# Second product of a two-layer block in seven quarter products, with v loaded through converting transfers

## The chip, the cores and the metric

The kernel runs on one core of a Trainium2 chip. A core has five engines that take their instructions in the order in which they were written and meet through semaphores: TensorE (PE in the profile; its weight loads are PEld), VectorE (DVE), ScalarE (ACT), GpSimd (POOL) and SyncE (SP), which here only issues transfers. The metric is the device time of one execution in microseconds (us). The kernel before took 211.14 us, the median of three runs (210.97 to 211.48).

## The reference, cut to what matters

A decayed linear attention over 4 sequences of 768 tokens with 8 heads of 64, in blocks of 64 tokens, and behind it a two-layer block (512 to 2048 to 512) with a sloped rectifier:

```
for b in range(nb):
    intra = einsum('bhic,bhjc->bhij', qb, kb) * Dmask
    intra = einsum('bhij,bhjd->bhid', intra, vb)
    inter = einsum('bhid,bhde->bhie', qb * lam_pow, kv_state)
    out[:, :, sl] = intra + inter
    kv_state = lam_block * kv_state + einsum('bhsd,bhse->bhde', kb * rev_pow, vb)
x = out.transpose(0, 2, 1, 3).reshape(B * S, H * D)     # 3072 x 512
h = x @ w_in                                            # 3072 x 2048
g = maximum(h, 0) + alpha * minimum(h, 0)
result = g @ w_out                                      # 3072 x 512
```

## The kernel before, in words

**Tiles.** The kernel works in blocks of 128 tokens instead of 64. The 3072 tokens are six chunks of 512 (two sequences by 256 tokens). Tokens of a chunk are kept by parity e (even or odd) and by sequence b, so a chunk is four groups of 128 tokens, (e, b). Attention is done in 24 units: unit n is a chunk, one of its two sequences, and one half of the heads, in that order, so units 8 to 11 belong to chunk 2 and units 16 to 19 to chunk 4.

**A unit's preparation.** `load` (line 80) brings k, q and v as fp32 into `raws`, `cast` (261) makes 16-bit copies, `key_decayed` (285) makes kdec = k times its decay, `transposes` with "D" (302) turns q and k in a transfer from SP, and `decayed` (346) makes qdT = turned q times its decay. For some units `load_v16` (272) brings v straight into 16 bits by a converting transfer that POOL issues.

**A unit's products** stand in `cluster(old, new)` (474). PE does `inter(old)` (4 products, which read qdT), `score_products(new)` (16), `intra(old)` (16, which read v16 and the masked scores) and `state_products(new)` (16 or 8, which read kdec and v16). Then DVE does `masked(new)` (398), ACT copies old's result to `XT`, which is the transposed x of the chunk (`attended`, 441), and DVE updates the state R (461). Each unit is new in one cluster and old in the next. `cluster2` (676) does the same for up to two old and two new units at once, with a second accumulator `acc2` in the PSUM bank "tk".

**The two-layer block.** `up(c, f)` (527) is one step of the first product: 4 matmuls of 512 columns give h for 128 of the 2048 hidden units and all 512 tokens of chunk c in a PSUM bank; ACT makes m = relu(-h) (540), DVE makes g = m * oma + h in fp16 (549). `down(c, t, part, 4)` (556) is a quarter of the second product for one 128-token group t: 4 matmuls of 512 columns, with g as the stationary operand and `w_out_sb` as the moving one. Behind the fourth part, `store` (573) copies the bank with ACT and writes 256 KB. A chunk has 16 ups and 16 downs.

**PSUM banks.** The 8 banks are acc (2), s (2), "op", "tk" and two that rotate under the name "h". Ups and downs name the bank they take. In the last stages ups take "h" alone, so an up can start only when DVE is done with the up two before.

**Order.** The emission order is written by hand. Lines 700 to 1003 interleave the ups and downs of chunks 0 to 2 with the preparation of units and with `cluster(n, n+1)` up to `cluster(15, 16)`. From line 1011 a `plan` gives for chunks 3, 4 and 5 a string of U (an up of that chunk) and D (a down of the chunk before), and at which step what else is emitted. I call these the stages of chunk 3, 4 and 5. Behind them `down_last` (580) does chunk 5's second product, with the last of its four groups cut into widths of 256, 128 and 128.

**Places that the steps below touch:** the clusters (11,12) in line 959 and (14,15) in line 991; the casts of v on ACT and POOL in lines 944 to 950, 966 and 998 to 1002; `key_decayed(12)` and `decayed(12)` in lines 937 and 938, the last work of POOL ahead of v of unit 13; the downs of chunk 1 in lines 915 to 930 and 987; the ups of chunk 2 from line 962; the plan; and `down_last`.

Of the kernel before, what the change touches and what calls it, by code (L numbers as in the profile page):

```python
# [11 lines left out]
def kernel(  # L12
# [16 lines left out]
    nc = tc.nc  # L29
# [9 lines left out]
    L = 128  # L39
# [10 lines left out]
    half_pool = ctx.enter_context(tc.tile_pool(name="half", bufs=4))  # L50
    kv_pool = ctx.enter_context(tc.tile_pool(name="kvh", bufs=8))
# [5 lines left out]
    o_pool = ctx.enter_context(tc.tile_pool(name="o", bufs=3))  # L57
# [22 lines left out]
    def load(c, bi, x, half=None, queue="S"):  # L80

        pb, b = c // 2, 2 * (c % 2) + bi
        if (c, bi) not in raws:
            raws[c, bi] = [raw_pool.tile([128, H, 2 * D], fp32, tag=f"{n}raw", name=f"{n}raw") for n in "kqv"]
        heads = ds(0, H) if half is None else ds(4 * half, 4)
        i = "kqv".index(x)
        (nc.gpsimd if queue == "G" else nc.sync).dma_start(
            out=raws[c, bi][i][:, heads, :],
            in_=(k, q, v)[i][b, heads, ds(pb * W, W), :].rearrange("h (p e) d -> p h (e d)", e=2),
        )  # L90
# [163 lines left out]
    def raw_of(n):  # L254
        c, bi, hh = units[n]
        return {
            x + "16": t[:, ds(4 * hh, 4), :].rearrange("p h (e d) -> p e h d", e=2)
            for x, t in zip("kqv", raws[c, bi])
        }

    def cast(n, name, eng):
        t = T.setdefault(n, {})
        if name == "v16":
            t[name] = kv_pool.tile([128, 4, 2, D], fp16, tag=name, name=name)
            c, bi, hh = units[n]
            copy_on(eng, t[name].rearrange("p h e d -> p h (e d)"), raws[c, bi][2][:, ds(4 * hh, 4), :])
            return
# [258 lines left out]

    def up(c, f, bi=None, bank="h"):
# [13 lines left out]
        if (c, f) not in G:  # L541
            G[c, f] = g_pool.tile([128, 2, 2, L], fp16, tag=f"g{f}", name=f"g{f}")
        g = G[c, f]
# [9 lines left out]
    def lhs(c, f, t):  # L553
        return G[c, f][:, t // 2, t % 2, :]
# [40 lines left out]
    acc2 = []  # L595

    def second():

        t = bank_of("tk", "acc2")
        nc.vector.memset(t[:, 256:512], 0.0)  # L600
        acc2.append(t)

    def out_of(i):
        x = [acc[:, 0, 0:256], acc[:, 1, 0:256]] if i == 0 else [acc2[0][:, 0:256], acc[:, 1, 256:512]]
        return [y.rearrange("p (h i) -> p h i", h=2) for y in x]

    def kv_of(i):
        return [kv_acc[0] if i == 0 else acc2[0][:, 256:512].rearrange("p (h l d) -> p h l d", h=2, l=2)]

    def inter_in(n, t, one_bank):  # L610
        co, bo, ho = units[n]
        pbo, bb = co // 2, 2 * (co % 2) + bo
        for a in range(2):
            for hp in range(2):
                nc.tensor.matmul(  # L615
                    t[a][:, hp, :].rearrange("p (e j) -> p e j", e=2),
                    lhsT=R[bb, ho, 2 * pbo + a][:, hp].rearrange("p l d -> p (l d)"),
                    rhs=T[n]["qdT"][:, :, hp, ds(a * 64, 64)],
                    start=(hp == 0 and not (one_bank and a == 1)),
                    stop=False,  # L620
                    skip_group_check=True,
                )

    def intra_in(n, t):
        for hp in range(2):
            for e in range(2):
                for hl, a in QUADS:
                    p = ds(a * 64, 64)
                    nc.tensor.matmul(  # L629
                        t[a][ds(hl * 64, 64), hp, :],  # L630
                        lhsT=T[n]["v16"][p, 2 * hp + hl, e, :],
                        rhs=T[n]["sm"][p, hl, hp, 1 - e, :],
                        start=False,
                        stop=(e == 1),
                        skip_group_check=True,
                    )

    def scores_in(n, s):
        t = T[n]
        for hp in range(2):  # L640
            for e in range(2):
                for a, hl in QUADS:
                    p = ds(hl * 64, 64)
                    nc.tensor.matmul(
                        s[hl][ds(a * 64, 64), hp, 1 - e, :].rearrange("p (e j) -> p e j", e=2),
                        lhsT=t["qkT"][p, 1, e, hp, ds(a * 64, 64)],
                        rhs=t["qkT"][p, 0, :, hp, ds(a * 64, 64)],
                        start=True,
                        stop=True,
                    )  # L650

    def masked_in(n, s):
        t = T[n]
        t["sm"] = sm_pool.tile([128, 2, 2, 2, L], fp16, tag="sm", name="sm")
        whole = mask_of(units[n][2])
        x = [list(y) for y in whole.ap]
        for hl in range(2):
            nc.vector.tensor_tensor(
                out=t["sm"][:, hl],
                in0=s[hl],  # L660
                in1=bass.AP(tensor=whole.tensor, offset=whole.offset + 384 * hl, ap=[x[0], [192, 2], x[2], x[3]]),
                op=ALU.mult,
            )

    def attended_in(n, t, eng):
        co, bo, ho = units[n]
        if co not in XT:
            XT[co] = xt_pool.tile([128, NHP, 2, 2, L], fp16, tag="xT", name="xT")
        x = XT[co][:, ds(2 * ho, 2), :, bo, :].rearrange("p h e (a j) -> p a (h e) j", a=2)
        if eng == "A":  # L670
            copy_on(eng, x, acc[:, :, 0:256].rearrange("p a (he j) -> p a he j", j=64))
        else:
            for a in range(2):
                copy_on(eng[a], x[:, a], t[a].rearrange("p h (e j) -> p (h e) j", e=2))

    def cluster2(olds, news):

        for i, n in enumerate(olds):
            inter_in(n, out_of(i), i == 1)
        if news:  # L680
            score_products(news[0])
        for i, n in enumerate(olds):
            intra_in(n, out_of(i))
        for i, n in enumerate(news):
            state_products(n, kv_of(i), i == len(olds))
        if len(news) == 2:
            s = [bank_of("h", "s2").rearrange("p (h x j) -> p h x j", h=2, x=2) for _ in range(2)]
            scores_in(news[1], s)
        if news:
            masked(news[0])  # L690
        if len(news) == 2:
            masked_in(news[1], s)
        for i, n in reversed(list(enumerate(olds))):
            attended_in(n, out_of(i), "A" if i == 0 else "AA")

    def states2(news):
        for i, n in enumerate(news):
            states(n, kv_of(i))
# [117 lines left out]
    load(4, 0, "v", 0)  # L816
# [275 lines left out]
```

## Time and profile before

| what | value |
|---|---|
| median of three runs | 211.14 us (210.97 to 211.48) |
| profiled execution, first to last instruction (span) | 209.1 us |
| TensorE clock granted, mean | 1.000 |
| matmul groups: up (line 532), down (562), last down (585) | 392, 320, 96 matmuls |
| data written to memory | 6.29 MB |

The profile shows one execution. The time of a run holds some two microseconds in addition to the span. Busy time of PE is from the start of a matmul to its modelled end; matmuls are pipelined, so the interval between two of them is shorter than the duration of one, and prices of PE work are taken from intervals. The chain of work is the sequence of instructions, followed back from the last one, each of which released the next. The timeline lists each engine's instructions in order of time, with neighbours of one kind merged: start, length, engine, line, operation and count.

### The profile page before, as it was taken

The numbers are of one execution on the slowest core, as the hardware profiler recorded it, in microseconds if no ns is written. First come the engines' busy times: TensorE is split into PE (matmuls) and PEld (weight loads), VectorE is DVE, ScalarE is ACT, GpSimd is POOL, SyncE is SP. The second block draws the span as 40 slices with busy tenths as digits, with TensorE's granted clock in tenths as the row PEclk, the third lists the DMA queues.
The fourth block names the chain that finished last, engine by engine and source line by source line (L and its number), as shares of the span: only waits on it lengthen the run. The fifth ranks groups of instructions, "written<-read, shape, count | busy, mean of one in ns | idle before, by whom it ended". The sixth has DMA issues, their size and how long they took to land.

```text
span 209.1 us, 5240 instructions
## 1 busy us (share of the span) xinstructions
PE 204.0 (98%) x2151; PEld 109.3 (52%) x2151; DVE 132.4 (63%) x233; ACT 110.8 (53%) x207; POOL 84.3 (40%) x114
## 2 busy tenths in 40 slices
PE   7999999999999999999999999999999999999993
PEld 6776455456445465555554464544544444444453
DVE  7978889488789466999956656744674344444000
ACT  7986778154876127666844544643454544344121
POOL 8999793052476983381902938022000000000000
PEclk9999999999999999999999999999999999999999
DMA  6999999998999998999199990404110100111113
GB/s 159 277 197 239 245 253 206 241 282 260 269 211 262 196 241 184 252 209 221 28 220 229 298 211 1 103 0 103 50 48 5 50 39 11 53 52 50 51 50 103
DMA packets 56716, 32.20 MB, mean 154 GB/s; under 512 B 22948, under 2 KB 53044, under 8 KB 56692
## 3 DMA queue, kind: packets, MB, share of 16 engines
q1 hardware_dynamic: 45764, 23.34, 46.4%
q0 software_dynamic: 10912, 8.52, 23.4%
q8 instruction: 17, 0.28, 0.6%
q14 instruction: 7, 0.06, 0.1%
q10 hardware_dynamic: 16, 0.00, 0.0%
HBM read 27.27 MB, written 6.29 MB: 161 GB/s over the span
## 4 chain that ended last, share of the span: by engine, by line
PE 92%; DVE 3%; ACT 2%; issue 1%; ACTq 0%
PE h_ps L532 39%; PE o_ps L562 33%; PE o_ps L585 7%; PE s L387 3%; PE acc L412 2%; PE tpx L337 2%; PE acc L371 2%; DVE dmask L200 1%; PE acc L432 1%; PE acc L629 1%; PE acc L615 1%; ACT qk L248 1%; ACT L178 1%; ACT xT L248 1%; DVE kdec L289 1%
## 5 line engine op out<-in xcount | busy, mean ns | idle before, releaser
L549 DVE SCALAR_TENSOR_TENSOR g<-m,oma,h_ps 128x512 f16<-128x512 f32 (+1 forms) x98 | 71.2, 736 | 46.3 <-ACT m L540 43.3
L532 PE MATMUL h_ps<-xT,w_in_sb 128*128 128x512 f16 (+1 forms) x392 | 91.4, 375 | 0.1
L540 ACT ACTIVATE m<-h_ps 128x512 f32<-128x512 f32 (+1 forms) x98 | 57.3, 588 | 51.0 <-PE h_ps L532 50.5
L562 PE MATMUL o_ps<-w_out_sb,g 128*128 128x512 f16 x320 | 79.0, 379 | 0.0
L532 PEld LDWEIGHTS <-w_in_sb 128*128 128x128 f16 x392 | 37.9, 98 | 43.6 <-issue 0.5
L562 PEld LDWEIGHTS <-g 128*128 128x128 f16 x320 | 29.9, 98 | 34.1 <-DVE g L549 0.2
L398 DVE TENSOR_TENSOR sm<-s,dmask 128x1024 f16<-128x1024 f32 x21 | 25.6, 1221 | 12.4 <-PE s L387 11.7
L351 POOL TENSOR_TENSOR qdT<-qkT,qdecay 128x512 f16<-128x512 f16 (+1 forms) x19 | 20.5, 1083 | 17.3 <-PE h_ps L532 7.2
L248 ACT ACTIVATE xT<-acc 128x512 f16<-128x512 f32 (+1 forms) x27 | 14.2, 550 | 22.6 <-PE acc L432 19.4
L575 ACT ACTIVATE o_sb<-o_ps 128x512 f32<-128x512 f32 (+2 forms) x26 | 14.7, 564 | 15.9 <-PE o_ps L585 10.9
L289 POOL TENSOR_TENSOR kdec<-kraw,kdecay 128x512 f16<-128x512 f32 x18 | 19.7, 1102 | 6.0 <-DMA kraw<-in_k_dram 6.0
L461 DVE SCALAR_TENSOR_TENSOR R<-R,rdecay,acc 128x128 f16<-128x128 f16 x54 | 15.3, 342 | 0.0
L252 POOL CAST qk<-qraw 128x512 f16<-128x512 f32 x12 | 7.4, 614 | 17.1 <-DMA qraw<-in_q_dram 16.2
L252 POOL CAST qk<-kraw 128x512 f16<-128x512 f32 x14 | 8.6, 614 | 13.9 <-DMA kraw<-in_k_dram 10.1
L585 PE MATMUL o_ps<-w_out_sb,g 128*128 128x512 f16 (+2 forms) x96 | 14.1, 308 | 0.0
L585 PEld LDWEIGHTS <-g 128*128 128x128 f16 x96 | 8.1, 98 | 6.1
L387 PE MATMUL s<-qkT 64*64 64x128 f16 x336 | 8.8, 221 | 0.1
L276 POOL DMA_DIRECT2D v<-in_v_dram x11 | 8.6, 792 | 0.0
L248 ACT ACTIVATE qk<-qraw 128x512 f16<-128x512 f32 x11 | 6.9, 624 | 2.7 <-DMA qraw<-in_q_dram 2.1
L252 POOL CAST v<-vraw 128x512 f16<-128x512 f32 x10 | 6.1, 615 | 5.4 <-DMA vraw<-in_v_dram 5.4
L387 PEld LDWEIGHTS <-qkT 64*64 64x64 f16 x336 | 5.8, 106 | 2.1 <-issue 0.4
L248 ACT ACTIVATE qkT<-tpx 128x512 f16<-128x512 f16 x11 | 6.5, 598 | 0.8 <-PE tpx L337 0.8
(76 smaller groups left out, 133.5 us busy)
## 6 DMA issues: line engine op xcount, KB each, us to landing
out_dram<-o_sb SPq DMA_DIRECT2D x23, 256.0 KB, 2.3
kraw<-in_k_dram SPq DMA_DIRECT2D x7, 512.0 KB, 5.6
qraw<-in_q_dram SPq DMA_DIRECT2D x6, 512.0 KB, 5.9
w_in_sb<-in_moe_w_in_dram POOLq DMA_DIRECT2D x4, 512.0 KB, 8.0
w_out_sb<-in_moe_w_out_dram POOLq DMA_DIRECT2D x4, 512.0 KB, 10.6
vraw<-in_v_dram SPq DMA_DIRECT2D x7, 256.0 KB, 5.7
qraw<-in_q_dram POOLq DMA_DIRECT2D x6, 256.0 KB, 7.2
qraw<-in_q_dram SPq DMA_DIRECT2D x6, 256.0 KB, 4.8
```

The source lines that it names most:

```text
L248: nc.scalar.activation(out, in_, AF.Copy)
L252: nc.gpsimd.tensor_copy(out=out, in_=in_)
L289: engine(eng).tensor_tensor(out=kdec, in0=kr, in1=kdecay[:, ds(4 * hh, 4), :].rearrange("p h e -> p e h").unsqueeze(3).to_broadcast([128, ...
L351: engine(eng).tensor_tensor(out=qdT[:, :, :, p], in0=(t["qps"] if eng == "P" else t["qkT"][:, 0])[:, :, :, p], in1=qdecay[:, hh, :, :, p], ...
L387: nc.tensor.matmul(t["s"][ds(a * 64, 64), hl, hp, 1 - e, :].rearrange("p (e j) -> p e j", e=2), lhsT=t["qkT"][p, 1, e, hp, ds(a * 64, 64)] ...
L398: nc.vector.tensor_tensor(out=t["sm"].rearrange("p a h x j -> p (a h) x j"), in0=t["s"].rearrange("p a h x j -> p (a h) x j"), in1=mask_of ...
L461: nc.vector.scalar_tensor_tensor(out=R[b, hh, m + 1][:, hp], in0=R[b, hh, m][:, hp], scalar=rdecay[:, 2 * hh + hp : 2 * hh + hp + 1], in1= ...
L532: nc.tensor.matmul(h_ps[:, 0:n] if bi is None else h_ps[:, 0:n].rearrange("p (e j) -> p e j", e=2), lhsT=w_in_sb[:, gi, ts(f, 128)], rhs=x ...
L540: nc.scalar.activation(m[:, 0:n], h_ps[:, 0:n], AF.Relu, scale=-1.0)
L549: nc.vector.scalar_tensor_tensor(out=g, in0=mv, scalar=oma[:, f : f + 1], in1=hv, op0=ALU.mult, op1=ALU.add)
L562: nc.tensor.matmul(o_ps, lhsT=lhs(c, f, t), rhs=w_out_sb[:, f, :], start=(f == 0), stop=(f == NF - 1),)
L585: nc.tensor.matmul(o_ps[:, 0:n], lhsT=lhs(c, f, t), rhs=w_out_sb[:, f, ds(x, n)], start=(f == 0), stop=(f == NF - 1),)
```

## The change

Chunks 2 to 5 form their second product from quarters. With A the 512 tokens by 2048 hidden values (rows cut by parity e, columns into f below 8 and from 8 on) and B the weights (rows cut likewise, columns into halves of 256), the scheme takes four sums of quarters of A, four sums of quarters of B, seven products instead of eight, and adds products in PSUM: a bank is read between two products that accumulate in it.

- **Sums of weights** (`weight_sum`): eight DVE instructions of 128x1024 fp16, two for each sum. Six are emitted among the first downs of chunk 1, two behind the last down of chunk 1. The last sum overwrites a quarter of `w_out_sb`.
- **Sums of g** (`g_sum`): sixteen instructions of 128x512 fp16 for each chunk. Sums 1 and 3 go to POOL (`sums13`) during the ups, 2 and 4 to DVE during the downs. In the last chunk the sums 2 are emitted behind the second part of product 1.
- **Products** (`product`): each of the seven has two parts (b), each of 8 matmuls with 256 moving columns. A D of the plan is now one such part, 14 for a chunk.
- **Readouts** (`evacuated`): four copies on ACT and three additions on DVE for a chunk, where four ACT copies stood.
- **Order:** ups of chunks 2 to 5 go by f = 0, 8, 1, 9 and so on. `cluster2` goes, and all units use `cluster`. The plan is one string for the chunks 3 to 5.
- **v:** the fp32 loads of v and the casts go. Where a cast of v stood, `load_v16` stands, on POOL.

```diff
-    o_pool = ctx.enter_context(tc.tile_pool(name="o", bufs=3))
+    o_pool = ctx.enter_context(tc.tile_pool(name="o", bufs=5))
...
     def casts(n, eng):
-        for name, e in zip(("k16", "q16", "v16"), eng):
+        for name, e in zip(("k16", "q16"), eng):
             cast(n, name, e)
+        load_v16(n)
         key_decayed(n)
...
+    def weight_sum(i, part):
+        p = ds(4 * part, 4)
+        (b11, b12), (b21, b22) = [[y[:, p] for y in x] for x in halves]
+        w = [w_sum[:, x, p] for x in range(3)]
+        out, in0, in1 = [(w[0], b12, b11), (w[1], b22, w[0]), (w[2], b21, w[1]), (b12, b22, b12)][i]
+        nc.vector.tensor_tensor(out=out, in0=in0, in1=in1, op=ALU.subtract)
...
+    def g_sum(c, i, j, eng):
+        a11, a12, a21, a22 = [part_of(c, j, half, e) for e in range(2) for half in range(2)]
...
+        out, in0, in1, op = {
+            1: (s1, a21, a22, ALU.add),
+            3: (a21, a11, a21, ALU.subtract),
+            2: (a11, s1, a11, ALU.subtract),
+            4: (a12, a12, a11, ALU.subtract),
+        }[i]
+        engine(eng).tensor_tensor(out=out, in0=in0, in1=in1, op=op)
+
+    CHAIN = [(1, 0), (2, 1), (6, 0), (5, 1), (7, 0), (3, 1), (4, 0)]
+
+    def product(c, i, b, t, fresh, last, cols):
+        for f in range(NF // 2):
+            x = sums[c][:, f, b] if i == 5 else g_of(c, f + 8 * (i in (2, 3, 4)))[:, int(i in (4, 7)), b]
...
+            nc.tensor.matmul(
+                t[:, cols],
+                lhsT=x,
+                rhs=w,
+                start=(fresh and f == 0),
...
+    def evacuated(c, i, key, t, b=None):
...
+        where = {2: ("c11", 0, 0), 3: ("c12", 0, 1), 4: ("c21", 1, 0), 7: ("c22", 1, 1)}
+        if i in (1, 5, 6, 4):
+            nc.scalar.activation(fresh({1: "c11", 5: "c22", 6: "c12", 4: "c21"}[i]), t, AF.Copy)
+        else:
+            o = X[where[i][0]]
+            nc.vector.tensor_tensor(out=o, in0=o, in1=t, op=ALU.add)
...
+    def down2(c, x):
+        i, side = CHAIN[x // 2]
+        b = x % 2
...
+        product(c, i, b, t, b == 0 and i in (1, 2, 5), i in (2, 3, 4) and b == 1, ds(256 * b, 256))
+        if b == 1:
+            evacuated(c, i, "w", t)
...
+    def down2_last(c):
+        order = [(i, side, b) for i, side in CHAIN[:5] for b in range(2)]
+        order += [(3, 1, 0), (4, 0, 0), (3, 1, 1), (4, 0, 1)]
...
+            product(c, i, b, t, i in (1, 2, 5), i in (2, 3, 4), ds(0, 256))
+            evacuated(c, i, b, t[:, 0:256], b)
+            if i == 1 and b == 1:
+                for j in range(4):
+                    g_sum(c, 2, j, "V")
...
+    def sums13(c, j, eng="G"):
+        g_sum(c, 1, j, eng)
+        g_sum(c, 3, j, eng)
...
     down(1, 1, 0, 4, "h")
+    weight_sum(0, 0)
     transposes(11, "D", False)
     down(1, 0, 0, 4, "tk")
+    weight_sum(0, 1)
...
     cluster(10, 11, "A")
-    load(3, 1, "v", 0)
-    cast(13, "v16", "A")
+    load_v16(13)
     down(1, 2, 2, 4, "h")
-    cast(12, "v16", "A")
+    load_v16(12)
     transposes(13, "D", False)
-    cast(15, "v16", "G")
+    load_v16(15)
...
     cluster(13, 14, "A")
     down(1, 3, 3, 4, "op")
+    weight_sum(3, 0)
+    weight_sum(3, 1)
+    up(2, 4, None, "h")
+    up(2, 12, None, "h")
+    up(2, 5, None, "op")
+    cluster(14, 15, "A")
...
+        3: {
+            0: lambda: (turned(18), load(5, 0, "k"), load(5, 0, "q"), decayed(17)),
+            2: lambda: prepared(19),
+            4: lambda: cluster(16, 17),
+            7: lambda: (turned(19), decayed(18)),
+            10: lambda: prepared(20),
+            11: lambda: cluster(17, 18),
...
+    order = "UU" + "DU" * 14
...
+                up(c, u // 2 + 8 * (u % 2), None, "h")
+                u += 1
+                if x in (17, 21, 25, 29):
+                    sums13(c, (x - 17) // 4)
             else:
-                down(c - 1, d // 4, d % 4, 4)
+                down2(c - 1, d)
+                for i, j in {1: [(2, 0), (2, 1)], 2: [(2, 2)], 3: [(2, 3)], 5: [(4, 0)], 6: [(4, 1)], 7: [(4, 2)], 8: [(4, 3)]}.get(d, []):
+                    g_sum(c - 1, i, j, "V")
                 d += 1
-    for t in range(4):
-        down_last(NC - 1, t, (DM,) if t < 3 else (256, 128, 128))
+    down2_last(NC - 1)
```

More of the change, by code (lines that the diff above doesn't have):

```diff
@@ L593, in down_last @@
             x += n
[L595 to L650, printed above, removed]
@@ L676, in cluster2 @@
[L676 to L694, printed above, removed]
```

211 lines of the change are left out of this document (106 added, 105 removed).

## The prediction

> **What bounds the kernel now.** I read the page's busy time and chain of work first, then the stretches by window, then the chain's pieces in order of time.
>
> ```profile
> PE 204.0 (98%) x2151; PEld 109.3 (52%) x2151; DVE 132.4 (63%) x233; ACT 110.8 (53%) x207; POOL 84.3 (40%) x114
> DVE  7978889488789466999956656744674344444000
> PE 92%; DVE 3%; ACT 2%; issue 1%; ACTq 0%
> ```
>
> TensorE sets the time: it is busy for 98% of the span and makes up 92% of the chain. DVE has room on average, but not everywhere: its row has four nines in slices 17 to 20. Each slice is 5.2 us, so these are about 84 to 105 us.
>
> ```profile
> 82.00:106.00 24.00, 23.94 (x293) 12.47 (x292) 22.58 (x43) 16.14 (x28) 12.56 (x15) 1.00 0.82 177
> 162.00:192.00 30.00, 30.00 (x169) 13.85 (x170) 12.81 (x18) 13.77 (x25) 0.00 (x0) 1.00 0.09 36
> ```
>
> These are a stretch's length, PE, PEld, DVE, ACT and POOL busy, clock, DMA share and GB/s. From 82 to 106 us, the first product of chunk 2, DVE works 22.58 of 24 us. From 162 to 192 us, where chunk 5's ups alternate with chunk 4's downs, it works 12.81 of 30. So whatever takes matmul columns away is gained, as long as nothing else becomes late, and the first of these stretches is where that is hardest.
>
> **What the seven products save.** From the chain (start, length) and from ACT in the timeline:
>
> ```profile
> 190.30 0.86 PE o_ps L562 x4
> 191.16 0.86 PE h_ps L532 x4
> 192.03 13.91 PE o_ps L585 x96
> 206.01 0.28 ACT o_sb L575
> ```
>
> ```profile
> 202.47 0.60 ACT L575 ACTIVATE o_sb<-o_ps 128x512 f32<-128x512 f32 x1 [2.91 <-PE o_ps L585]
> 204.22 0.38 ACT L575 ACTIVATE o_sb<-o_ps 128x256 f32<-128x256 f32 x1 [1.15 <-PE o_ps L585]
> 205.12 0.28 ACT L575 ACTIVATE o_sb<-o_ps 128x128 f32<-128x128 f32 x1 [0.51 <-PE o_ps L585]
> ```
>
> A down and an up last 0.864 us each, 216 ns for a matmul of 512 columns. The three copies mark the ends of the 512, 256 and 128 wide pieces of the last group: 16 matmuls of 256 columns took 204.22 - 202.47 = 1.75 us, 109.4 ns each. A chunk's second product is now 16 x 0.864 = 13.82 us. It becomes 14 parts of 8 matmuls, 112 x 109.4 ns = 12.25 us. Chunks 2 to 4 save 3 x 1.57 = 4.71 us, and the last second product, 13.91 us in the chain, saves 1.66. **Together -6.4 us**, on an engine that is never idle.
>
> **Clusters, one at a time.**
>
> ```profile
> 86.42 0.22 PE acc L371 x4
> 87.34 0.97 PE o_ps L562 x4
> 123.22 0.45 PE acc L615 x8
> 124.93 1.83 PE o_ps L562 x8
> ```
>
> `cluster` with one old and one new unit takes 0.92 us of PE (86.42 to 87.34), `cluster2` with two and two 1.71 (123.22 to 124.93), or 0.86 for a pair. The last stages handle 7.5 pairs: 7.5 x 0.06 us, **+0.5 us**.
>
> **v of unit 12.** `cluster(11, 12)` reads it in its state products. Today ACT casts it from data long loaded. The change issues its transfer on POOL, in order behind `decayed(12)` and the transfer for unit 13.
>
> ```profile
> 75.89 1.16 POOL L351 TENSOR_TENSOR qdT<-qkT,qdecay 128x512 f16<-128x512 f16 x1
> 76.99 0.61 POOL L252 CAST v<-vraw 128x512 f16<-128x512 f32 x1
> ```
>
> ```profile
> L276 POOL DMA_DIRECT2D v<-in_v_dram x11: 752/780/912, 5.1 to 60.7; - x11
> DMA to landing us min/median/max: 4.9/6.4/11.2
> ```
>
> ```profile
> 80.84 0.29 PE L432 MATMUL acc<-v,kdec 64*64 64x64 f16 x16
> ```
>
> The cast that follows `decayed(12)` starts at 76.99, so today's POOL would issue unit 13's transfer there and unit 12's 0.78 later. Two things move this. Without the loads of v on SP, a wait of POOL for q at 67.96 shrinks (below). Against it, six weight sums on DVE fall into 69 to 75 us, beside POOL's own work:
>
> ```profile
> 67.96 0.61 POOL L252 CAST qk<-qraw 128x512 f16<-128x512 f32 x1 [1.70 <-DMA qraw<-in_q_dram]
> 68.53 1.90 POOL L289 TENSOR_TENSOR kdec<-kraw,kdecay 128x512 f16<-128x512 f32 x1
> 44.53 1.04 POOL L289 TENSOR_TENSOR kdec<-kraw,kdecay 128x512 f16<-128x512 f32 x1 [1.04 <-DMA kraw<-in_k_dram]
> ```
>
> ```profile
> 68.84 0.69 DVE L289 TENSOR_TENSOR kdec<-kraw,kdecay 128x512 f16<-128x512 f32 x1
> 44.56 1.30 DVE L250 CAST qk<-kraw 128x512 f16<-128x512 f32 x1
> 36.46 0.41 DVE L250 COPY qkT<-tpx 128x512 f16<-128x512 f16 x1
> ```
>
> The POOL product takes 1.04 us by itself and 1.90 when DVE's product of two SBUF operands runs inside it. The DVE cast beside a POOL product takes 1.30, and a DVE copy of that size out of PSUM 0.41. So the two engines delay each other by up to one instruction. The wait for q can give back 1.7 us at most, and six sums of about 0.6 us (next part) can cost 3.7. I take +1.0: unit 12's transfer starts at 76.99 + 1.0 + 0.78 = 78.8. The shortest landing of the eleven, 4.9 us, fits best, as the queue is then shorter than on average: 83.7 against 80.84, and I take **+2.7 us**. A quiet queue or an earlier issue ends it at 0; the full 3.7 us of delay and the median landing would make it 76.99 + 3.7 + 0.78 + 6.4 - 80.84 = 7.0. PE waits there in the middle of a cluster, and everything behind it on PE waits too.
>
> **Sums of weights behind the last down of chunk 1.** Two sums of 128x1024 fp16 enter DVE's busiest stretch. The price is not in the trace. Nearest rows:
>
> ```profile
> 35.52 0.68 DVE L289 TENSOR_TENSOR kdec<-kraw,kdecay 128x512 f16<-128x512 f32 x1
> 36.12 0.42 DVE L351 TENSOR_TENSOR qdT<-qkT,qdecay 128x256 f16<-128x256 f16 x1
> ```
>
> ```profile
> L250 DVE COPY qkT<-tp 128x1024 f16<-128x1024 f16 x1 | 0.7, 686 | 0.0
> ```
>
> The next instruction starts 0.60 us after the product of 512 (36.12 - 35.52), which has an fp32 operand, and 0.34 after that of 256: 1.12 for 1024 at this rate. Copies of fp16 alone took 0.41 for 512 and 0.69 for 1024, and the next one starts 0.08 before such a row ends (35.52 + 0.68 against 36.12). That gives 0.34 and 0.61. These are the two ends; I take the copies' rate, as all operands of the new sums are fp16 too.
>
> ```profile
> 94.40 2.40 DVE L549 SCALAR_TENSOR_TENSOR g<-m,oma,h_ps 128x512 f16<-128x512 f32 x3
> 96.71 1.22 DVE L398 TENSOR_TENSOR sm<-s,dmask 128x1024 f16<-128x1024 f32 x1
> 97.84 1.11 DVE L461 SCALAR_TENSOR_TENSOR R<-R,rdecay,acc 128x128 f16<-128x128 f16 x4
> 98.88 2.72 DVE L549 SCALAR_TENSOR_TENSOR g<-m,oma,h_ps 128x512 f16<-128x512 f32 x4
> 103.15 0.74 DVE L549 SCALAR_TENSOR_TENSOR g<-m,oma,h_ps 128x512 f16<-128x512 f32 x1
> ```
>
> ```profile
> 100.77 0.98 PE h_ps L532 x4
> ```
>
> From 94.40 to 103.9 DVE hardly rests, so 2 x 0.61 us make all that follows late. The g of chunk 2's last up ends at 105.1 instead of 103.9 and the g of chunk 3's first up at 105.9. The third up of chunk 3 needs that bank. Counted from 100.77, three ups and a down later, it would start at 104.2. **+1.7 us** (0.4 if the sums were free, 2.7 at the upper price, 4.8 if each also met a POOL product).
>
> **Sums of g in stages 3 to 5.** Product 6 starts with the fifth D and reads sum 2 of its last group in its seventh matmul. DVE makes that sum behind the g of the up before and the addition that reads product 2.
>
> ```profile
> 192.70 0.75 DVE L549 SCALAR_TENSOR_TENSOR g<-m,oma,h_ps 128x512 f16<-128x512 f32 x1 [0.98 <-ACT m L540]
> ```
>
> The last up ends at 192.03 (191.16 + 0.86) and its g starts 0.67 later. Call the end of such an up 0: its g takes DVE to 1.42, the addition (priced as g, 0.75) to 2.17, the sum to 2.51. PE has a D, an up and six matmuls to do, 0.87 + 0.86 + 0.66 = 2.39, less 0.2 for the weight load ahead. So PE waits about 0.35 us, once in each stage. In the stage of chunk 3, POOL is occupied by `prepared(19)`, `decayed(17)` and the late sums 1 and 3, and DVE's four sums and POOL delay each other: I add 0.8 (0, or 3.4 if each of the four met a whole product of 1.04 and 0.8 of that were absorbed). **+1.15, +0.35, +0.35 us.** The other sums and the four ACT copies have several D of cover; if DVE fell a microsecond behind, they would be late next.
>
> **The end.** Behind the last up, g (to 1.43), two POOL sums of 1.04 and a DVE sum of 0.34 must pass before product 6's seventh matmul at 3.5 + 0.66 - 0.2 = 3.96 us: about even, up to 1 us late when DVE's sums stretch POOL's. The last piece has 256 columns instead of 128, a copy of 0.38 instead of 0.28 us and twice the bytes. **+0.5 us** together (0.2 to 1.2).
>
> **Sum.** -6.4 + 0.5 + 2.7 + 1.7 + 1.15 + 0.7 + 0.5 = +0.85 us on the profiled 209.1. The median of the runs stands 2.04 above the span, so 211.14 + 0.85 = **212.0 us**. The additions are of the size of the gain, and I do not know their sign better than that.
>
> **Rivals.**
>
> *v lands in time.* The place is the state products of `cluster(11, 12)` at 80.84, the price is the 2.7 us, and it decides when unit 12's transfer is issued before 76 (with 4.9 us of landing). For it speaks that POOL's wait of 1.70 for q gets shorter, as the loads of v on SP go; against it, the weight sums beside POOL. Not slower, but faster: **209.3 us**.
>
> *Everything hides.* v lands, and the DVE sums cost PE nothing but the lag of 0.4 at the third up and the 0.35 of each stage: 209.3 - 1.3 - 0.8 - 0.3 = **206.9 us**. Against it stands DVE's 22.58 of 24 us.
>
> *DVE and POOL block each other.* Each DVE sum of two SBUF operands meets a POOL product, and one of them pays: 2.3 us more at `cluster(11, 12)`, 1.0 more at the weight sums, 1.6 more in the stage of chunk 3: **216.9 us**. For it: the rows of 1.90 and 1.30 us. Against it: the DVE product inside the 1.90 took 0.69, no more than alone, and POOL is busy for 12.56 of the 24 us from 82 to 106, so not each sum meets it. [...]
>
> *Halving the columns saves nothing,* because the weight loads, one for each matmul, set the pace: then a chunk's second product stays at 13.8 us and the time is 212.0 + 6.4 = **218.4 us**. Against it: the 128 wide pieces, also with a load each, took 205.12 - 204.22 = 0.90 us for 16, 56 ns. [...]
>
> **Chances.** Forecast (211.0 to 214) 0.35; v in time 0.27; everything hides 0.13; blocking 0.21; no saving on PE 0.04. About 0.3%, 0.6 us, is what a measurement of this kernel can tell from no change. Faster: 0.13 + 0.27 = 0.40. The same: 0.11, the forecast's lower part. Slower: 0.49. The range leaves out the last case and the outer ends of "hides" and "blocking": 206.5 to 217.5 us. By itself the forecast has 211 to 214.
>
> **What would show it.** Right: 256 wide matmuls at 109 ns intervals; a gap of PE in the middle of `cluster(11, 12)` that ends with the landing of v; a wait of PE at the third up of chunk 3 that ends with DVE's g; a short wait at product 6 of each chunk that ends with DVE's sum. Wrong: PE without gaps from 75 to 115 us (then 207), or gaps that end with POOL's sums 1 and 3, or with v of unit 17, whose transfer also stands late in POOL's order.

## The result and the profile after

The changed kernel takes 220.49 us (median, 217.51 to 220.88), beside 211.08 for the kernel before on the same chip: ratio 1.0405, interval 1.0336 to 1.0473. It is slower, and 3 us above the upper end of the range. The profiled execution has a span of 218.3 us, 9.2 more than before.

The page of the changed kernel, the same rows as before: busy time, DVE's slices, the granted clock by slice, and the chain.

```profile
PE 201.9 (92%) x2311; PEld 127.8 (59%) x2311; DVE 166.1 (76%) x284; ACT 110.0 (50%) x203; POOL 129.7 (59%) x149
DVE  7988889287889974999965879757879548585840
PEclk9999999999999999999996999999999999999999
PE 68%; DVE 9%; POOL 6%; issue 6%; DMA 6%; ACT 3%; ACTq 0%; SPq 0%; DVEq 0%; POOLq 0%
```

PE works less than before (201.9 us after 204.0), but idles for 16.4 us of the span, where it idled for 5.1. DVE has 34 us more work and POOL 45. The chain, 92% PE before, is PE for 68% only. The row of the clock has one slice at 6, the 22nd, about 115 to 120 us.

PE's timeline, only its waits and what follows the longest: start, length, instruction, count, and in brackets the idle time before it and what ended it.

```profile
78.34 0.38 PE L368 MATMUL acc<-qdT,R 128*128 128x128 f16 x4 [2.06 <-DVE R L458]
...
84.31 0.32 PE L429 MATMUL acc<-v,kdec 64*64 64x64 f16 x16 [1.41 <-DMA v<-in_v_dram]
...
101.32 3.61 PE L538 MATMUL h_ps<-xT,w_in_sb 128*128 128x512 f16 x16 [1.53 <-DVE g L553]
...
108.71 1.04 PE L643 MATMUL o_ps<-w_out_sb,g 128*128 128x256 f16 x8
110.40 1.02 PE L538 MATMUL h_ps<-xT,w_in_sb 128*128 128x512 f16 x4 [0.66 <-DVE g L553]
...
115.37 0.31 PE L429 MATMUL acc<-v,kdec 64*64 64x64 f16 x8 [3.16 <-DMA v<-in_v_dram]
115.62 1.89 PE L643 MATMUL o_ps<-w_out_sb,g 128*128 128x256 f16 x8
117.30 1.88 PE L538 MATMUL h_ps<-xT,w_in_sb 128*128 128x512 f16 x4
119.00 1.04 PE L643 MATMUL o_ps<-w_out_sb,g 128*128 128x256 f16 x8
...
120.75 1.04 PE L643 MATMUL o_ps<-w_out_sb,g 128*128 128x256 f16 x8
121.62 1.03 PE L538 MATMUL h_ps<-xT,w_in_sb 128*128 128x512 f16 x4
...
123.76 0.39 PE L643 MATMUL o_ps<-w_sum,g 128*128 128x256 f16 x2 [0.45 <-DVE g L626]
...
145.17 1.02 PE L538 MATMUL h_ps<-xT,w_in_sb 128*128 128x512 f16 x4 [0.60 <-DVE g L553]
...
155.42 0.39 PE L643 MATMUL o_ps<-w_sum,g 128*128 128x256 f16 x2 [0.60 <-DVE g L626]
...
176.49 1.02 PE L538 MATMUL h_ps<-xT,w_in_sb 128*128 128x512 f16 x4 [0.60 <-DVE g L553]
...
206.40 1.60 PE L643 MATMUL o_ps<-w_sum,g 128*128 128x256 f16 x12 [0.46 <-DVE g L626]
```

From here the 9.2 us can be put together. A D, eight matmuls of 256 columns, takes 121.62 - 120.75 = 0.87 us, as forecast, so PE's -6.4 stands; the clusters' +0.5 is taken over as forecast. The ten waits sum to 11.5 us. The D at 115.62 and the up at 117.30 take 119.00 - 115.62 = 3.38 us instead of 0.87 + 0.86, another 1.65. That makes 7.3. PE also loses a little more at each wait than the brackets say: the D at 108.71 is through at 109.58, the next up starts at 110.40, 0.82 later and not 0.66. If each of the ten waits costs some 0.16 more, as this one does, that is 1.6 (an estimate), which makes 8.9 of the 9.2.

Three places carry most of it, and none of them has a term in the sum of the prediction: `cluster(10, 11)` at 78.34, v of unit 17 at 115.37, and the slow stretch behind it.

**At cluster(10, 11)** PE waits for the state R of the cluster before. DVE's timeline of the changed kernel shows why:

```profile
70.98 5.05 DVE L609 TENSOR_TENSOR w_sum<-w_out_sb,w_sum 128x1024 f16<-128x1024 f16 x4
75.95 1.21 DVE L395 TENSOR_TENSOR sm<-s,dmask 128x1024 f16<-128x1024 f32 x1
77.09 1.10 DVE L458 SCALAR_TENSOR_TENSOR R<-R,rdecay,acc 128x128 f16<-128x128 f16 x4
```

Four sums of weights take 5.05 us, 1.26 each, and the masking and R of the cluster stand behind them. POOL casts and multiplies without a pause at that time. How much room DVE had is in its timeline of the kernel before:

```profile
73.61 1.22 DVE L398 TENSOR_TENSOR sm<-s,dmask 128x1024 f16<-128x1024 f32 x1 [3.42 <-PE s L387]
```

DVE rested for 3.42 us ahead of this masking, and R was done at 75.86 for a cluster that PE began at 76.44, so some 4.0 us were to spare. Six sums at the prediction's 0.61 us would have fitted. The six as they ran held DVE for 6.2 us (69.12 to 70.32 and 70.98 to 75.95), 2.2 too much, about the wait.

The first two of them ran beside a cast of POOL, in DVE's and POOL's timelines of the changed kernel:

```profile
69.12 1.28 DVE L609 TENSOR_TENSOR w_sum<-w_out_sb 128x1024 f16<-128x1024 f16 x2
68.44 2.43 POOL L253 CAST qk<-qraw 128x512 f16<-128x512 f32 x1 [0.86 <-DMA qraw<-in_q_dram]
```

Here POOL paid, 2.43 us for a cast that takes 0.61 elsewhere, although it had started first, and the two sums took 0.68 each, as they do where POOL waits. Beside the other four both paid: two casts of POOL took 1.07 and two qdT 1.60, where 0.61 and 1.16 are usual.

**At 115.37** the chain in order of time (start, length, what) runs through transfers:

```profile
98.70 6.04 DMA kraw<-in_k_dram
...
104.81 1.05 POOL kdec L285
105.86 1.11 POOL s L626
...
109.27 6.06 DMA v<-in_v_dram
...
115.37 0.31 PE acc L429 x8
```

POOL stands still for a load of k, then makes kdec, two sums of g and a qdT, and only then issues v of unit 17 (109.27), which lands 6.06 us later.

**Behind that wait** the clock falls. The stretches by window of the changed kernel (length, five engines' busy time, granted clock, DMA share, GB/s):

```profile
114.00:116.00 2.00, 0.63 (x10) 0.48 (x10) 0.00 (x0) 0.28 (x1) 1.98 (x4) 0.90 1.17 322
116.00:118.00 2.00, 2.00 (x10) 1.22 (x8) 1.65 (x3) 0.78 (x2) 2.00 (x3) 0.50 1.97 221
118.00:120.00 2.00, 2.00 (x12) 1.19 (x11) 1.46 (x3) 0.74 (x2) 1.98 (x3) 0.75 1.15 106
```

PE gets half its clock (0.50 granted from 116 to 118 us) from about the end of the wait to about 119 us and pays 1.65 us beyond the wait itself.

### The profile page after: what moved, and what is told of

The parts are those of the page before. It is cut to its first block, busy times and chain, and to the rows that moved or that the text cites. A ratio compares the mean times of both kernels' runs of the same rounds, so it can differ in the third digit from the quotient of the medians.

```text
span 218.3 us, 5673 instructions
## 1 busy us (share of the span) xinstructions
PE 201.9 (92%) x2311; PEld 127.8 (59%) x2311; DVE 166.1 (76%) x284; ACT 110.0 (50%) x203; POOL 129.7 (59%) x149
## 4 chain that ended last, share of the span: by engine, by line
PE 68%; DVE 9%; POOL 6%; issue 6%; DMA 6%; ACT 3%; ACTq 0%; SPq 0%; DVEq 0%; POOLq 0%
PE h_ps L538 29%; PE o_ps L643 20%; PE o_ps L566 7%; DMA v<-in_v_dram 3%; DMA kraw<-in_k_dram 3%; DVE w_sum L609 3%; PE s L384 3%; PE unread L151 2%; PE acc L409 2%; PE tpx L334 2%; DVE g L626 2%; ACT m L546 2%; DVE g L553 2%; POOL s L626 2%; PE acc L368 2%
## 5 line engine op out<-in xcount | busy, mean ns | idle before, releaser
L643 PEld LDWEIGHTS <-g 128*128 128x128 f16 x384 | 37.2, 99 | 14.6 <-DVE g L626 2.9
L626 POOL TENSOR_TENSOR s<-g 128x512 f16<-128x512 f16 x16 | 18.8, 1175 | 39.6 <-PE o_ps L643 24.2
L643 PE MATMUL o_ps<-w_out_sb,g 128*128 128x256 f16 x256 | 33.2, 277 | 0.0
L249 ACT ACTIVATE xT<-acc 128x512 f16<-128x512 f32 x24 | 14.3, 597 | 31.8 <-PE acc L429 29.4
L566 PE MATMUL o_ps<-w_out_sb,g 128*128 128x512 f16 x128 | 30.4, 380 | 0.0
L626 POOL TENSOR_TENSOR g<-g 128x512 f16<-128x512 f16 x16 | 19.1, 1197 | 1.3
L272 POOL DMA_DIRECT2D v<-in_v_dram x24 | 18.8, 787 | 0.0
L643 PE MATMUL o_ps<-w_sum,g 128*128 128x256 f16 x128 | 17.2, 273 | 1.5 <-DVE g L626 1.5
L566 PEld LDWEIGHTS <-g 128*128 128x128 f16 x128 | 11.4, 98 | 12.0 <-DVE g L553 0.2
L673 ACT ACTIVATE o_sb<-o_ps 128x512 f32<-128x512 f32 (+1 forms) x20 | 10.2, 512 | 14.1 <-PE o_ps L643 13.6
L626 DVE TENSOR_TENSOR g<-s,g 128x512 f16<-128x512 f16 x16 | 10.8, 704 | 0.0
```

Source lines behind the costliest of these rows:

```text
L272: nc.gpsimd.dma_start(out=v16.rearrange("p h e d -> p h (e d)"), in_=v[2 * (c % 2) + bi, ds(4 * hh, 4), ds((c // 2) * W, W), :].rearrange( ...
L566: nc.tensor.matmul(o_ps, lhsT=lhs(c, f, t), rhs=w_out_sb[:, f, :], start=(f == 0), stop=(f == NF - 1),)
L626: engine(eng).tensor_tensor(out=out, in0=in0, in1=in1, op=op)
L643: nc.tensor.matmul(t[:, cols], lhsT=x, rhs=w, start=(fresh and f == 0), stop=(last and f == NF // 2 - 1), skip_group_check=True,)
```

## The experiments

Theory A: a few waits, each curable by itself (v of units 12 and 17, the sums of weights and of g), make the time. Theory B: POOL and DVE are so full that behind each cured wait the next one takes its place. A sharper form came up on the way, theory L: DVE and POOL hold each other up, an instruction at a time, wherever a DVE sum meets POOL's work. Ratios are to the kernel before on the same chip.

| run | us, median (range) | ratio, 95% interval |
|---|---|---|
| v_early | 219.91 (217.09 to 221.18) | 1.038 (1.0294 to 1.0467) |
| ws6_early | 215.4 (214.8 to 216.0) | 1.0211 (1.0162 to 1.026) |
| before_v | 211.71 (211.15 to 212.16) | 1.0042 (1.0019 to 1.0066) |
| no_sums | 207.57 (207.42 to 208.47) | 0.9849 (0.9803 to 0.9895) |
| v_ws8 | 213.27 (212.89 to 214.83) | 1.0138 (1.0097 to 1.0179) |
| no_13 | 209.22 (208.44 to 210.57) | 0.9937 (0.9915 to 0.9958) |
| no_24 | 208.88 (208.68 to 209.58) | 0.9921 (0.9898 to 0.9944) |
| all_v | 215.83 (215.21 to 219.13) | 1.0233 (1.0209 to 1.0256) |
| five | 212.59 (212.08 to 212.78) | 1.0073 (1.0053 to 1.0094) |
| five_spread | 211.74 (210.57 to 212.92) | 1.0036 (1.0013 to 1.006) |
| five_spread_aa | 208.16 (207.07 to 208.86) | 0.9858 (0.9829 to 0.9887) |
| v17_early | 222.09 (217.03 to 222.91) | none |
| ws6_v17 | 215.06 (214.54 to 218.59) | 1.0206 (1.0184 to 1.0228) |
| v_ws8_aa | 214.51 (213.04 to 216.96) | 1.0157 (1.0116 to 1.0197) |

### v_early: transfers of v earlier

```diff
     load_v16(10)
+    load_v16(12)
+    load_v16(13)
...
     load_v16(16)
+    load_v16(17)
+    load_v16(18)
```

> The changed kernel, with the transfers of v for units 12 and 13 issued behind that of unit 10, and those for units 17 and 18 behind that of unit 16; nothing else moves. Theory A (single waits, each with its own cause): the waits of PE for v in the clusters (11,12) and (16,17), 1.6 and 3.2 us in the changed kernel's trace, and the slower clock behind the second, some 1.7 us, go: 213 to 215 us. Theory B (POOL and VectorE are simply full, so that the next wait takes the place of the one taken away): no more than 2 us are gained, 218 us or more.

The time is theory B's. Both waits for v are gone, but PE's timeline shows others, here the first of them:

```profile
78.78 0.41 PE L368 MATMUL acc<-qdT,R 128*128 128x128 f16 x4 [2.07 <-DVE R L458]
...
80.33 3.78 PE L566 MATMUL o_ps<-w_out_sb,g 128*128 128x512 f16 x12
```

The same wait as in the changed kernel (2.06 there), but now with a slow clock behind it: 12 matmuls that last 2.76 us otherwise take 3.78. The dip that stood behind v of unit 17 has moved here, and a second one stands behind 1.98 us of waiting for g at 102 us. So the mechanism is only in part theory B's: the waits of this execution are 2.3 us shorter in all (9.2 after 11.5), but two slow stretches cost it some 3.1 us where one cost 1.65. Its executions lie 4 us apart, so its median says little.

### ws6_early: six sums of weights at 39 us

```diff
     decayed(5, "V")
+    weight_sum(0, 0)
...
+    weight_sum(2, 1)
```

> The changed kernel, with the six sums of weights that stand among chunk 1's first downs moved to the rest of VectorE near 39 us, where POOL waits for data too. Theory A: each sum takes 0.6 us there instead of 1.26, PE's wait of 2.1 us ahead of cluster (10,11) goes, and POOL reaches v of unit 12 some 3 us earlier, so the wait of 1.6 there goes too; the wait for v of unit 17 stays: 216 to 217 us. Theory B: at most 1 us less, 219 us.

Theory A was right here as to the time: 5.1 us less than the changed kernel by the medians (4.1 by the ratios), a little better than expected. In the traces 2.1 us less at `cluster(10, 11)`, 0.9 and 1.9 less at the two waits for v, and 1.65 less at the clock stand against 1.1 more at an up and 1.45 more at product 6. The rows of the four sums that read an earlier sum (minimum, median and maximum in ns, first and last start), first in the changed kernel:

```profile
L609 DVE TENSOR_TENSOR w_sum<-w_out_sb,w_sum x4: 1092/1270/1646, 71.0 to 74.9; 128x1024 f16<-128x1024 f16 x4
```

and in ws6_early, where POOL sits waiting for q at that time:

```profile
L609 DVE TENSOR_TENSOR w_sum<-w_out_sb,w_sum x4: 682/684/684, 40.0 to 41.8; 128x1024 f16<-128x1024 f16 x4
```

The same instruction takes 0.68 us where POOL waits and 1.09 to 1.65 beside POOL's work. Other traffic is no rival: PE works without a pause in both places, and transfers move more where the sums are short, 258 GB/s in the slice of ws6_early's page from 37.4 to 42.8 us beside 155 GB/s at 71 to 75 us of the changed kernel. This is theory L, seen directly.

### before_v: the kernel before with converting transfers alone

```diff
-    load(3, 1, "v", 0)
-    cast(13, "v16", "A")
+    load_v16(13)
...
-    cast(12, "v16", "A")
+    load_v16(12)
```

> The kernel before with one part of the change alone: every v by a converting transfer where its cast stood, no fp32 loads of v, second products as before. Theory A: v of unit 12 is late by 1 to 2 us in cluster (11,12), all else is in time: 212 to 213 us. Theory B: no change, 211 us, as POOL and VectorE have no sums to make.

The transfers alone cost 0.9 us (0.0042 of 211), between the two forecasts. PE's one wait later than 60 us is in `cluster(11, 12)`, where the prediction put it, but shorter:

```profile
81.76 0.32 PE L433 MATMUL acc<-v,kdec 64*64 64x64 f16 x16 [0.80 <-DMA v<-in_v_dram]
```

### no_sums: seven products without any sum

All sums of weights and of g are left out, and the products read the quarters themselves.

> The changed kernel without any sums of weights and of g; the products read the unsummed quarters, so the second product of chunks 2 to 5 is not what the reference computes. Theory A: the seven products save their 6.4 us of TensorE time, the clusters cost 0.5, and with POOL free v comes nearly in time: 205 to 207 us. A rival that puts the loss into the products themselves (matmuls of 256 columns, the readouts midway, the banks): 211 us or more.

The span is 205.6 us, 3.5 below before, with 2.1 us of waits still in it (0.55 for v of unit 12, 0.39 and twice 0.60 at the third ups of stages), so the time is just above the 207 of theory A. So the saving on PE is real, and the rival by which weight loads set the pace falls.

### v_ws8: both cures together

The fourth sum of weights gets its own tile, so that all eight can be early.

```diff
-    w_sum = const.tile([128, 3, NF // 2, 256], fp16, name="w_sum")
+    w_sum = const.tile([128, 4, NF // 2, 256], fp16, name="w_sum")
...
+    weight_sum(3, 0)
+    weight_sum(3, 1)
```

> v of units 12, 13, 17 and 18 is issued earlier, and all eight sums of weights are made at about 39 us, behind decayed(5). The fourth sum of weights gets a tile of its own, and for the room o_pool has 4 buffers and kv_pool 7. The whole product is computed. Theory A (single waits, and a clock that falls only behind a wait of 2 us or more): against the kernel with six early sums (215.4) the waits for v of units 12 and 17 go (0.51 + 1.26) and those for the two late sums of weights (1.34 + 0.66); what is left is the sums of g: 212 to 213.5, mean clock 1.000, no stretch of PE below full clock. Theory B (POOL and DVE are full, so the next wait takes the place of each one removed): 214.5 or more, with sums of g on DVE ending longer waits than the 1.9 us seen there.

The time is theory A's: 213.27. Theory B's sign is there too, a wait for a sum of g longer than 1.9 us. Most of what is left in the stage of chunk 3 stands at product 6, in PE's timeline:

```profile
114.23 0.39 PE L643 MATMUL o_ps<-w_sum,g 128*128 128x256 f16 x2 [0.62 <-DVE g L626]
...
116.82 0.39 PE L643 MATMUL o_ps<-w_sum,g 128*128 128x256 f16 x2 [2.20 <-DVE g L626]
```

The cause is in DVE's timeline, two late sums of 2.36 and 1.41 us, where the median of these sums is 0.43:

```profile
111.15 0.73 DVE L553 SCALAR_TENSOR_TENSOR g<-m,oma,h_ps 128x512 f16<-128x512 f32 x1
111.81 2.36 DVE L626 TENSOR_TENSOR g<-s,g 128x512 f16<-128x512 f16 x1
...
115.36 1.41 DVE L626 TENSOR_TENSOR g<-s,g 128x512 f16<-128x512 f16 x1
```

and in POOL's timeline of the same moments:

```profile
111.71 1.06 POOL L285 TENSOR_TENSOR kdec<-kraw,kdecay 128x512 f16<-128x512 f32 x1
112.72 1.17 POOL L348 TENSOR_TENSOR qdT<-qkT,qdecay 128x512 f16<-128x512 f16 x1
113.82 0.82 POOL L253 CAST qk<-kraw 128x512 f16<-128x512 f32 x1
```

POOL's kdec began 0.1 us ahead of DVE's sum. The sum's length fits standing still through kdec and, behind it, through qdT; it ended 0.35 us after qdT's successor began. POOL's two products took their usual 1.06 and 1.17, and the cast behind them 0.82 instead of 0.61: here DVE paid nearly alone, and through two of POOL's instructions. Which of the two began first doesn't settle who pays: POOL's kdec began ahead of DVE's sum here, and DVE paid; the sum at 115.36 began 0.05 us ahead of POOL's next kdec, 115.41, and still took 1.41; and the cast of 2.43 us above began 0.68 us ahead of DVE's first sum (68.44 and 69.12), and POOL paid.

### no_13 and no_24: half of the sums of g

Both are v_ws8 without POOL's sums 1 and 3, or without DVE's sums 2 and 4.

```diff
     def sums13(c, j, eng="G"):
-        g_sum(c, 1, j, eng)
-        g_sum(c, 3, j, eng)
+        return
```

> The kernel with early v and eight early sums of weights, but POOL's sums 1 and 3 of g are left out (product 5 and sum 2 read a quarter of g in the place of sum 1), so the output isn't the reference's. DVE's sums 2 and 4 stay. Theory L (DVE and POOL hold each other up, an instruction at a time): DVE's sums take 0.42 us each and no longer 0.65 to 0.70, PE's waits for them nearly go: 207.5 to 209. Theory D (DVE by itself has too much to do at product 6): the waits of 0.4 to 0.6 us in each stage stay: 209.5 or more.

```diff
+        if i in (2, 4):
+            return
         engine(eng).tensor_tensor(out=out, in0=in0, in1=in1, op=op)
```

> The kernel with early v and eight early sums of weights, but DVE's sums 2 and 4 of g are left out (products 3, 6, 4 and 7 read quarters of g in their place), so the output isn't the reference's. POOL's sums 1 and 3 stay. Theory L: POOL's sums get shorter than 1.18 us on average, and PE's waits go as well: 207.5 to 209, about as without POOL's sums, as either side alone does no harm. Theory P (POOL by itself has too much to do, its 37.9 us of sums on top of 84): waits for v, kdec or qdT in stage 3 stay: 210 or more.

Leaving out POOL's half gains 4.0 us and leaving out DVE's 4.4, though no_sums, without either (and without the sums of weights, but with v late), stands only 5.7 below v_ws8: the two halves cost something together that neither costs alone. DVE's sums in no_13:

```profile
L626 DVE TENSOR_TENSOR g<-g x32: 410/418/1521, 109.8 to 197.6; 128x512 f16<-128x512 f16 x32
```

The mean is 0.49 us (0.64 and 0.79 for the two kinds in v_ws8), but one sum still meets POOL's kdec (1.52 us), and PE waits 1.28 for it. So no_13 ends a little above the band of theory L, and no_24 within it. One part of theory L's forecast for no_24 fails: POOL's sums have a mean of 1.16 us there and 1.17 in v_ws8, so POOL loses next to nothing at these sums.

### all_v: all sums of g on DVE

```diff
-    def sums13(c, j, eng="G"):
+    def sums13(c, j, eng="V"):
```

> The kernel with early v and eight early sums of weights, but POOL's sums 1 and 3 of g are made by DVE too, at the same places. The whole product is computed. Theory L: the sums cost DVE 0.42 us each, 8 more for a chunk, 3.4 us in some 30 us, and POOL's rows get short again: 210 to 212.5, faster than the kernel it is made from. Theory D: DVE gets behind where chunk 2's sums stand beside its first product, and in each stage: 214 or more.

A miss for theory L, right for theory D: 215.83, and PE waits for DVE's g (2.44 us at the longest) and R (0.85) while chunk 2's sums stand beside its first product. DVE has no room for more work at each of these places; and its sums of g, priced at 0.42 us each, have means of 0.51 to 0.56 us by kind. Here moving work off POOL onto DVE didn't help.

### five, five_spread, five_spread_aa: a better order

Product 5 goes ahead of product 6, so that sum 2 has two more D's of time (the sums 2 are also emitted one behind each of four D's, where two stood behind the first); then the ups are spread; then ACT casts k of five units.

```diff
-    CHAIN = [(1, 0), (2, 1), (6, 0), (5, 1), (7, 0), (3, 1), (4, 0)]
+    CHAIN = [(1, 0), (2, 1), (5, 1), (6, 0), (7, 0), (3, 1), (4, 0)]
```

> The kernel v_ws8 with product 5 ahead of product 6, so that sum 2 has two more D's before it is read (ACT copies product 2, DVE then adds product 1 from the bank in which it waits; sums 1 and 3 of the next chunk start one step earlier, as product 5 is done earlier). The whole product is computed. Theory L (what is left of the loss is that DVE's sums 2 stand beside POOL's work and come late at product 6; it is a matter of the lead alone): the waits at product 6 go (0.62 + 2.20 in the stage of chunk 3, 0.46 at the end): 209.5 to 210.8. Theory B (DVE has no room, the lag turns up elsewhere, at the next up or the next cluster): 212.5 or more.

The waits at product 6 are gone, but theory B has the number: 212.59. DVE's late sums now delay g, in DVE's and PE's timelines of five:

```profile
111.01 4.03 DVE L626 TENSOR_TENSOR g<-s,g 128x512 f16<-128x512 f16 x1
115.76 1.02 PE L538 MATMUL h_ps<-xT,w_in_sb 128*128 128x512 f16 x4 [0.84 <-DVE g L553]
```

Two more such waits, 0.66 and 0.74 us, follow. The sum of 4.03 us is longer than POOL's kdec, qdT and cast of v_ws8 together (1.06, 1.17 and 0.82 us), and v_ws8's sum of 2.36 us lasted through the first two. So theory L's "an instruction at a time" is too mild: a DVE sum can last through several.

```diff
+        if c > 3:
+            order = "DU" * 5 + "U" + "DU" * 5 + "U" + "DU" * 4
```

> The kernel five, and in the stages of chunks 4 and 5 no three ups follow each other: the two ups without a D of their own stand behind the fifth and the tenth D, no longer ahead of the first. The whole product is computed. If the two waits of 0.60 us at the third up of these stages are a matter of two banks for three ups in a row, they go and nothing comes in their place: 1.2 us below five. If they are DVE's lag, they return at another up: within 0.4 us of five.

0.85 us less in the medians, with intervals that overlap. In the traces the two waits of 0.60 at the third up of the stages of chunks 4 and 5 are gone; one of 0.45 at another up came. So they were a matter of three ups in a row on two banks; how much of the 1.2 us is gained is not settled.

```diff
-        casts(n, "GA")
+        casts(n, "AA")
```

> The kernel five_spread, and the five casts of k of units 19 to 23 are made by ACT (0.4 to 0.6 us each) and not by POOL (0.6 to 0.8 each). The whole product is computed. Theory L: POOL's rows beside DVE's sums get fewer, DVE's sums 2 of chunk 2 shorter than 2.36 us at the longest; PE gains only what still waits for sums or units, 0 to 0.8 us. Rival: the casts make ACT's m of the ups late and PE waits at banks: up to 1 us slower.

208.16 us: 3.6 less than five_spread, more than forecast, and **1.4% faster than the kernel before** (0.9858, 0.9829 to 0.9887), with the whole result computed. Late in the stage of chunk 3 two waits for g are left (earlier in it 0.39 us for g and 0.68 for qdT):

```profile
117.82 1.02 PE L538 MATMUL h_ps<-xT,w_in_sb 128*128 128x512 f16 x4 [0.25 <-DVE g L553]
...
120.46 1.02 PE L538 MATMUL h_ps<-xT,w_in_sb 128*128 128x512 f16 x4 [0.74 <-DVE g L553]
```

and from 136 us on PE never rests:

```profile
136.00:166.00 30.00, 30.00 (x332) 20.53 (x331) 23.11 (x36) 15.59 (x27) 13.67 (x12) 1.00 0.20 50
166.00:196.00 30.00, 30.00 (x215) 20.77 (x213) 20.71 (x32) 12.90 (x24) 11.70 (x10) 1.00 0.13 45
```

The profiled execution, the longest of its six, has a span only 1.7 us below five_spread's, so the traces show half of the 3.6; the rest is not shown. The longest sum 2 takes 2.82 us there instead of 4.03, without a cast on POOL behind it.

### v17_early and ws6_v17: what is v of unit 17 worth?

Both issue v of units 17 and 18 behind that of unit 16, the first in the changed kernel, the second in ws6_early.

> The changed kernel, and only the transfers of v of units 17 and 18 are issued earlier, behind that of unit 16. Theory A (the 3.16 us for v of unit 17 stand by themselves, and the half clock behind them, about 1.7 us, is their consequence): 215.5 to 217, no stretch of half clock near 116 us. Theory B (POOL is full, and its lag turns up at sums 1 and 3 or at kdec): 218.5 or more.

Inconclusive. Its executions lie 6 us apart, too far for a ratio. The traced one waits at `cluster(10, 11)`, which is ahead of the edit and has the changed kernel's code:

```profile
81.37 0.58 PE L368 MATMUL acc<-qdT,R 128*128 128x128 f16 x4 [4.87 <-DVE R L458]
```

4.87 us here and 2.06 there: the same meeting of DVE and POOL can go well or badly. The six sums held DVE for 8.1 us here and 6.2 there.

> The changed kernel with the six sums of weights behind decayed(5) and, on top, the transfers of v of units 17 and 18 behind that of unit 16. Without the sums of weights beside POOL, the wait at cluster(10, 11) can't blur the effect of v of unit 17. Theory A (the wait for v of unit 17, 1.26 us with the early sums alone, is one by itself): 213.8 to 214.6, no wait for v of unit 17. Theory B (the next POOL product is late in its place): 215.2 or more.

215.06, within the noise of ws6_early's 215.4 and between the two bands, nearer to theory B's. The wait for v of unit 17, 1.26 us in ws6_early, is gone, and DVE is late in its place, in PE's timeline of ws6_v17:

```profile
115.70 1.02 PE L538 MATMUL h_ps<-xT,w_in_sb 128*128 128x512 f16 x4 [2.38 <-DVE g L553]
118.08 0.39 PE L643 MATMUL o_ps<-w_sum,g 128*128 128x256 f16 x2 [0.71 <-DVE g L626]
```

So this wait is no price that is saved when v is early: two sums 2 beside POOL, 4.06 us in DVE's timeline there, are late next. What the 3.16 us of the changed kernel are worth by themselves no run shows.

### v_ws8_aa: the casts without the order

> The kernel v_ws8 (product 6 third, as in the change), and the five casts of k of units 19 to 23 on ACT instead of POOL. The whole product is computed. Theory L (the sums 2 of chunk 2 are late because POOL's rows hold DVE up): the 0.62 + 2.20 us at product 6 shrink to 1.5 or less: 210.3 to 212. Rival (the gain of the kernel five_spread_aa came from its other edits or needs them): 213 or more.

A miss for theory L: 214.51, not below v_ws8, and two sums 2 that take 4.65 us together. In its trace kdec and qdT of the next unit only come sooner on POOL and meet the sums all the same. The casts gained on top of five_spread and nothing here. That they need the longer lead of sum 2 is likely but not shown; which of the two edits of five and five_spread they need was not tried.

## Why the prediction was wrong

The stretch of the kernel before in which the change puts six sums of weights (length, busy time of PE, PEld, DVE, ACT and POOL, clock, DMA share, GB/s):

```profile
70.00:82.00 12.00, 12.00 (x199) 6.71 (x198) 5.86 (x13) 4.43 (x8) 8.85 (x12) 1.00 1.00 196
```

- **PE's saving, -6.4 us:** right. 0.87 us for a D, and 207.57 us without the sums.
- **Clusters one at a time, +0.5:** not measured alone; the ledger above closes with it.
- **v of unit 12, +2.7:** right place and mechanism, too large. 1.41 us in the changed kernel, 0.80 in before_v. In the changed kernel the transfer was issued at some 80.4 us (the second of four from 79.67) instead of 78.8, but the cluster was late too.
- **Two sums of weights behind chunk 1's last down, +1.7:** near, 1.53 + 0.66 = 2.2, and in part by luck. The two sums took 2.71 us together beside POOL, not the 1.22 assumed, and the first part came already at an up of chunk 2.
- **Sums of g at product 6, +1.15, +0.35, +0.35, and +0.5 at the end:** mechanism right; 0.45, 0.60 and nothing. At the end 0.46 of waiting; the span beyond the last up fell by 0.8 us (218.3 - 202.0 after 209.1 - 192.0), where -1.66 + 0.5 was forecast.
- **The step that failed** is the one on the six early sums of weights: "against it, six weight sums on DVE fall into 69 to 75 us, beside POOL's own work". It asked only what they do to POOL, and so to v of unit 12. What they do to DVE itself, and so to R and `cluster(10, 11)`, has no term, and no reason is given. DVE had 5.86 of 12 us to do there, but POOL had 8.85; four of the six sums took 1.09 to 1.65 us instead of 0.68, R stood behind them, and PE waited 2.06 us for it. Moving these six instructions alone brought 5.1 us by the medians (4.1 by the ratios), with what they cost POOL.
- **v of unit 17** had no term, though the last paragraph named it as a sign. It cost 3.16 us, plus 1.65 at half clock, for which the prediction had no step at all.
- **Three ups in a row** at the start of a stage, two waits of 0.60 us, were taken as free.
- **The rivals:** the one that two engines block each other had the mechanism. It put their losses at an instruction each, in the places already counted, and not at R behind the six sums of weights; hence 216.9.

Open: which of the gains in ws6_early follow from which, since the wait at `cluster(10, 11)`, the half clock and v of unit 17 move each other; and why POOL's instructions keep their length in some meetings (1.06 and 1.17 us in v_ws8) and stretch in others (2.43 us for a cast in the changed kernel).

## What to carry to other kernels

Price a new DVE instruction like the sums here (two fp16 operands in SBUF) not by its own duration but by what POOL does at that time, and place it where POOL waits: a sum of weights took 0.68 us there and 1.09 to 1.65 beside POOL's work. When a chain engine loses its cover, a cured wait often only uncovers the next one; look for what else is due at the same moment on the same pair of engines before trusting a sum of single waits. A gap on TensorE can cost more behind it: 1.65 us behind the 3.16 us of the changed kernel, some 1.5 each behind the 2.07 and 1.98 of v_early, and nothing behind 2.38 in ws6_v17.

## What the hardware showed beyond that

The clock. In the changed kernel a granted clock of 0.50 followed a wait of 3.16 us and lasted from 115.6 to about 119.0, 3.4 us. In v_early it followed waits of 2.07 and of 1.98, each time for 3.4 us too (79.0 to 82.4 and 102.9 to 106.3, reckoned from the clock of windows of 2 us), while 2.06 us at the same place of the changed kernel, 2.20 in v_ws8 and 2.38 in ws6_v17 left the clock at 1.00. So a wait of 1.98 us was enough and one of 2.38 was not: these runs show no length of a wait at which the clock falls, and the 2 us in the expectation of v_ws8 was its author's estimate. Why equal waits differ no run here tests.
